# Attention and feed-forward on one core: two sets of scores at a chunk's end, a softmax one slot sooner, an output block added by GpSimd

## The chip, the core and the metric

The kernel runs on one NeuronCore of a Trainium2 chip. Its engines are TensorE (PE, with its weight loads as PEld), VectorE (DVE), ScalarE (ACT), GpSimd (POOL) and SyncE (SP), which issues most of the DMAs. Each engine works through its own instructions in order. The metric is the device time of one execution in microseconds (us), the median over runs.

## What is computed

```python
block, window = (32, 16)
k_sum = k.reshape(B, H, nb, block, D).max(axis=3)
v_sum = v.reshape(B, H, nb, block, D).mean(axis=3)
scores_l = scale * np.matmul(q, k.transpose(0, 1, 3, 2))
mask_l = np.abs(pos[:, None] - pos[None, :]) < window
scores_s = scale * np.einsum('bhsd,bhnd->bhsn', q, k_sum) + np.log(block)
a = softmax(concat(where(mask_l, scores_l, -1e9), scores_s))
x = matmul(a, concat(v, v_sum))        # then heads side by side: 3072 x 512
h = np.maximum(x @ w_in, 0.0)
out = h * h @ w_out                    # 512 -> 2048 -> 512
```

There are 4 batches, 8 heads, 768 positions and a head size of 64, all in fp32. Each query sees its neighbours within 16 positions and one key and value for each block of 32.

## The kernel before

The 3072 tokens are 24 tiles of 128. Two tiles make a chunk of 256 tokens, so there are 12 chunks. A chunk's attention gives x (two halves, high and low part of each number), and the feed-forward of the chunk runs while the attention of the next chunk's two tiles, called a and a + 1, is made beside it.

The program has three parts. A START table of tokens, written out by hand, orders the work of the first chunks. Chunks 2 and 3 run through `slot` and `period`. Chunks 4 to 11 run through `chunk_blocks`, which holds most of the change.

`chunk_blocks(c)` has 8 slots, k = 0 to 7. A slot computes two 128-wide pieces of the first layer on PE (`ffn1`, L419, 24 matmuls into `ph`), then the second layer for the slot two before (`ffn2_blocks`, L650, 21 matmuls). The second layer uses a scheme with seven products in place of eight; its operands are made by `squares_blocks` (relu L427 and square L660 on ACT, L662 on ACT, L664 to L670 on POOL, L671 on DVE) and `split_blocks` (L675 on ACT, L676 on POOL). POOL also issues the loads of the summed weights into a ring (`load_t`, L619).

Beside this the lists `early[k]` and `late[k]` put attention steps into the slots. They run ahead of and behind `split_blocks` of their slot:

- `scores(g)` (L288): 16 matmuls of a 64x64 array form, each in two passes, into banks 0 and 1 of PSUM, for each tile g from 10 on the same two banks.
- `mask_max(g, h)` (L316, DVE): adds the mask to head h's scores, keeps the maximum, writes `e_sb`. Eight heads.
- `exponentials` (L324, ACT), `sharpen` and `norm` (L341, L351, L356, DVE), `turn` (L369, DVE): softmax and transposes into `pT`.
- `outputs(g)` (L387): 16 matmuls of 64 columns into `ph`'s banks, each in two passes; `high_x` (L401, ACT) and `low_x` (L404, DVE) split the result into x. `split_x` is both.
- `load_qk`, `load_v`, `place_k` bring the keys, queries and values of later tiles.

At a chunk's end `outputs` of both tiles and `scores` of the next chunk's first tile run, then the last two `ffn2_blocks`, and then `evict_blocks` adds the seven products into four output blocks (ACT copies one operand, DVE adds, SP stores). The scratch for it is `c11`, `c22`, `c12`, `c21`, which lie in the tiles `k_sb[0]` and `q_sb[0]`. `s_flat` is the tile `q_sb[2]`.

Of the kernel before, what the change touches and what calls it, by code (L numbers as in the profile page):

```python
# [20 lines left out]
B, H, S, D = 4, 8, 768, 64  # L21
# [11 lines left out]
FROM_BLOCKS = 4  # L33
# [33 lines left out]
SU14v F1.11.0 SH15 AD15 RE10a MU10 E5.0 CA15a SU15v F1.11.1 E5.2 E5.3 SQ10 GL10 F2.10.0 F2.10.1 RE11v SQ11 MU11 GL11  # L67
F2.11.0 F2.11.1 EP5.0v TT5.7 L:kw3 TT5.6 RE12a MU12 VT3 E5.7 SQ12 NR5.0p GL12 E5.5 F1.14.0 E5.6 L:q6 EP5.1p NR5.1v
N5.1v KT3 L:v5 L:kw0 L:v4 L:q7 L:k7 F1.15.0 EV2.0a L:o0 F1.14.1 N5.0p RE13a SQ13 MU13 EV2.1v L:o1 F2.12.0 GL13 TU5.2
RE14v TU5.0 MU14 F2.12.1 F2.13.0 F1.15.1 F2.13.1 SQ14 KT0 RE15a PK6a GL14 F2.14.0 F2.14.1 VT0 TU5.1 O5 O4 XH5 XL5 MU15  # L70
PK7a XH4 SQ15 XL4 GL15 S6.0 S6.1 S7.0 S7.1
"""


# [1 line left out]
def attn_ffn_kernel(ctx: ExitStack, tc: tile.TileContext, q, k, kt, v, vt, v0, w, consts, out, out_rows):  # L76
# [231 lines left out]
    def mask_max(g, h):  # L308

        t = g % NT  # L310
        m = mask_sb[:, 0 if t == 0 else 2 if t == NT - 1 else 1, :]
        half, i = divmod(h, 4)
        if (g, half) not in nmx:
            nmx[g, half] = work.tile([P, 4], F32, name="nmx", tag="nmx", bufs=7)
            sm[g, half] = work.tile([P, 4], F32, name="sm", tag="sm", bufs=7)
        nc.vector.tensor_tensor_reduce(  # L316
            out=e_of(g)[:, h, 0:NK], in0=s_ps[g][h % 2][:, h // 2, 0:NK], in1=m, scale=-scale, scalar=3.0e38,
            op0=ALU.add, op1=ALU.min, accum_out=nmx[g, half][:, i : i + 1],
        )

    def exponentials(g, h):
        half, i = divmod(h, 4)
        e = e_of(g)[:, h, 0:NK]
        nc.scalar.activation(  # L324
            e, e, AF.Exp, bias=nmx[g, half][:, i : i + 1], scale=-1.0, accum_out=sm[g, half][:, i : i + 1]
        )

    def softmax(g, h0, h1):

        for h in range(h0, h1):  # L330
            mask_max(g, h)
            exponentials(g, h)
# [21 lines left out]
    def norm(g, half, eng):  # L354
        e = e_of(g)[:, half * 4 : half * 4 + 4, 0:NK]
        eng.tensor_mul(out=e, in0=e, in1=sm.pop((g, half)).unsqueeze(2).to_broadcast([P, 4, NK]))  # L356
# [21 lines left out]
    def outputs(g):  # L378
        if g < FROM_PAIRS:
            held["O", g] = free.pop(0)  # L380
        xp = bank[held["O", g] if g < FROM_PAIRS else 5 - g % 2 if g < 2 * FROM_BLOCKS + 2 else 4 + g % 2]
        x_ps[g] = xp = xp.rearrange("a (p k) -> a p k", p=NPAIR)

        for s in range(2):
            for h in range(H):
                o = (h % 2) * 64
                nc.tensor.matmul(  # L387
                    xp[o : o + 64, h // 2, s * 64 : s * 64 + 64],
                    lhsT=v_sb[g % 2][:, s, h * 64 : h * 64 + 64],
                    rhs=pT[g % 2][:, h, s * 64 : s * 64 + 64],  # L390
                    start=True, stop=True,
                )
# [7 lines left out]
    def high_x(g):  # L400
        nc.scalar.copy(out=x_part(xh, "xh", g), in_=x_ps[g])  # L401

    def low_x(g):
        nc.vector.tensor_sub(out=x_part(xl, "xl", g), in0=x_ps.pop(g), in1=x_part(xh, "xh", g).bitcast(F32))  # L404
        if g < FROM_PAIRS:
            free.append(held.pop(("O", g)))

    def split_x(g):
        high_x(g)
        low_x(g)  # L410
# [114 lines left out]
    def sharpen(g, half):  # L525
        add_eps(g, half, nc.vector)
        inverse(g, half)
# [150 lines left out]
    def evict_blocks(c):  # L678


        mid, side = ob_last
        c11, c22, c12, c21 = side[:, 0:CT], side[:, CT:], mid[:, 0:CT], mid[:, CT:]
        o = (c - FROM_BLOCKS) * CT
        to = [out_rows[at : at + P, x : x + CT] for at in (o + P, o) for x in (0, CT)]
        x1, x2 = ([acc[i][:, h * CT : (h + 1) * CT] for h in range(2)] for i in (1, 2))
        x0, x3 = [acc[0][:, h * CT : (h + 1) * CT] for h in range(2)], acc[3][:, 0:CT]
        nc.scalar.copy(out=c21, in_=x1[1])
        nc.vector.tensor_add(out=c11, in0=x1[0], in1=c21)
        nc.sync.dma_start(out=to[0], in_=c11)
        nc.vector.tensor_add(out=c22, in0=x0[0], in1=c21)  # L690
        nc.vector.tensor_add(out=c21, in0=x0[1], in1=c22)
        nc.vector.tensor_add(out=c22, in0=x2[0], in1=c22)
        nc.vector.tensor_add(out=c12, in0=x2[1], in1=c22)
        nc.sync.dma_start(out=to[1], in_=c12)
        nc.vector.tensor_add(out=c22, in0=x3, in1=c22)
        nc.sync.dma_start(out=to[3], in_=c22)
        nc.vector.tensor_add(out=c21, in0=x3, in1=c21)
        (nc.scalar if c == n_c - 1 else nc.sync).dma_start(out=to[2], in_=c21)

    def chunk_blocks(c):  # L700
        a = 2 * c + 2
        more, next_too = a < n_g, a + 2 < n_g
        b, t = divmod(a, NT)
        early, late = [[] for _ in range(SLOTS)], [[] for _ in range(SLOTS)]
        if more:
            for h in range(2):
                early[0] += [lambda h=h: sharpen(a, h), lambda h=h: norm(a, h, nc.vector)]
            late[0].append(lambda: turn(a, 0, 3))
            early[1].append(lambda: turn(a, 3, 6))
            late[1] += [lambda: turn(a, 6, 7), lambda: load_v(a), lambda: load_v(a + 1)]  # L710
            early[2].append(lambda: turn(a, 7, 12))
            late[3] += [lambda h=h: mask_max(a + 1, h) for h in range(H)]
            for n in range(2):
                early[4 + n] += [lambda h=h: exponentials(a + 1, h) for h in range(4 * n, 4 * n + 4)]
            for h in range(2):
                early[4 + h] += [lambda h=h: sharpen(a + 1, h), lambda h=h: norm(a + 1, h, nc.vector)]
            late[5].append(lambda: turn(a + 1, 0, 5))
            early[6].append(lambda: turn(a + 1, 5, 9))
            late[6].append(lambda: turn(a + 1, 9, 12))
            if c == FROM_BLOCKS:  # L720
                for p in range(1, 4):
                    late[2 * p - 2].append(lambda p=p: load_kv(3, p))
                    (late[2], early[4], late[6])[p - 1].extend([lambda p=p: sum_k(3, p), lambda p=p: sum_v(3, p)])
            if b and t == 0:
                late[4] += [lambda: place_v(a, nc.scalar), lambda: place_v(a + 1, nc.scalar)]
            if next_too:
                late[3].append(lambda: load_qk(a + 2))
                late[4].append(lambda: load_qk(a + 3))
                late[5].append(lambda: place_k(a + 2, nc.scalar))
                late[6].append(lambda: place_k(a + 3, nc.scalar))  # L730
        for k in range(SLOTS):
            n = (c - FROM_BLOCKS) * SLOTS + k
            ph = bank[4 + k % 2]
            for i in range(2):
                ffn1(c, 2 * k + i, ph[:, i * CT : (i + 1) * CT])
            if n == 0:
                done = finish()
            if k == 3 and more:
                scores(a + 1, 0, NPAIR)
            if k > 1:  # L740
                ffn2_blocks(n - 2)
            squares_blocks(n, ph)
            if k > 1:
                load_t(n if n < SLOTS else n + 1)
            if n == 0:
                for h in range(2):
                    evict(*done, h, nc.scalar)
                    store(done[0], h)
                load_t1(SLOTS - 1)
            for do in early[k]:  # L750
                do()
            if k == SLOTS - 1 and more:
                outputs(a)
                outputs(a + 1)
                high_x(a)
            split_blocks(n)
            for do in late[k]:
                do()
        if more:
            if next_too:  # L760
                scores(a + 2, 0, NPAIR)
            low_x(a)
            split_x(a + 1)
            if next_too:
                softmax(a + 2, 0, H)
        ffn2_blocks(n - 1)
        ffn2_blocks(n)
        if n < SLOTS:
            load_t(n + 1)
        load_t(n + 2)  # L770
        load_t(n + 3)
        evict_blocks(c)
# [228 lines left out]
```

## Time and profile before

| what | us |
|---|---|
| median of 3 runs | 587.94 (587.77 to 588.04) |
| the profiled execution | 588.17 |
| its span, first to last instruction | 586.4 |
| PE busy in it | 573.3 |
| DVE, ACT, POOL busy | 397.1, 336.9, 361.1 |

The granted TensorE clock was full through the span. The span starts with the first instruction and ends with the last; the execution's own time has 1.8 us more around it. A busy share is an average over the parts of the program. What sets the time is read from the places where one engine waits for another, and from the chain of work that ended last, of which PE is 89%. A timeline row gives the start of a group of equal instructions, its length from first start to last end, the engine, the line and the shapes. Matmuls overlap each other by a little, so the spacing of two groups is read from their starts.

### The profile page before, as it was taken

What the parts mean: (1) busy time and instruction counts of PE and PEld (TensorE: products, weight loads), DVE (VectorE), ACT (ScalarE), POOL (GpSimd) and SP (SyncE); (2) the same over time, 40 slices, a digit from 0 to 9 for tenths busy, and PEclk for the clock granted to TensorE, in tenths of its full rate; (3) what the DMA queues carried; (4) which work ended last, traced back from release to release, by engine and by line L of the source; (5) the groups of instructions that cost most, each with busy time, mean ns of one, the idle gap of its engine ahead of it and who ended that gap; (6) DMA issues with size and microseconds to landing.
All of it is one profiled execution on the core that took longest, in us unless ns stands there. A gap on an engine that the chain in (4) does not pass through costs nothing.

```text
span 586.4 us, 15654 instructions
## 1 busy us (share of the span) xinstructions
PE 573.3 (98%) x6239; PEld 563.5 (96%) x6239; DVE 397.1 (68%) x1087; ACT 336.9 (57%) x822; POOL 361.1 (62%) x430
## 2 busy tenths in 40 slices
PE   7899999999999999999999999999999999999996
PEld 6789999999999999999999999999999999999996
DVE  6899797969978946676665665764756656655212
ACT  3898857345445536565575664565475575573552
POOL 2646644405776765764874874873875784675684
PEclk9999999999999999999999999999999999999999
DMA  8999800654467658978647556646656655455362
GB/s 297 371 345 414 355 2 10 222 174 164 162 206 234 195 159 257 301 253 300 203 157 240 194 176 201 208 169 213 212 172 199 219 201 163 150 192 172 104 212 92
DMA packets 42986, 121.23 MB, mean 207 GB/s; under 512 B 3936, under 2 KB 20320, under 8 KB 41376
## 3 DMA queue, kind: packets, MB, share of 16 engines
q1 hardware_dynamic: 31376, 67.66, 33.0%
q0 software_dynamic: 11392, 52.43, 27.4%
q8 instruction: 49, 0.80, 0.5%
q14 instruction: 25, 0.20, 0.1%
q10 hardware_dynamic: 144, 0.13, 0.1%
HBM read 105.53 MB, written 14.68 MB: 205 GB/s over the span
## 4 chain that ended last, share of the span: by engine, by line
PE 89%; DMA 6%; POOL 1%; DVE 1%; ACT 1%; SPq 1%; issue 0%; DVEq 0%; POOLq 0%
PE ph L419 39%; PE o_ps L464 15%; PE o_ps L650 15%; PE s_ps L650 10%; PE ph L387 4%; DMA v_sb<-in_v 3%; PE s_ps L288 3%; PE s_ps L419 3%; DMA t_ring<-t 1%; DMA c_sb<-in_consts 1%; POOL sets L676 0%; POOL q_sb L664 0%; PE s_ps L387 0%; POOL q_sb L670 0%; SPq L190 0%
## 5 line engine op out<-in xcount | busy, mean ns | idle before, releaser
L419 PE MATMUL ph<-x,w_sb 128*128 128x256 f32 x1848 | 220.6, 275 | 0.0
L419 PEld LDWEIGHTS ph<-x,w_sb 128*128 128x128 f32 x1848 | 214.6, 188 | 0.3 <-issue 0.3
L671 DVE TENSOR_TENSOR sets<-r,sets 128x384 fp32r<-128x384 f32 x64 | 49.7, 777 | 99.6 <-ACT sets L662 99.5
L369 DVE STREAM_TRANSPOSE pT<-e_sb 32x256 f32<-32x256 f32 x228 | 99.6, 437 | 4.0
L676 POOL TENSOR_TENSOR sets<-q_sb,sets 128x512 fp32r<-128x512 f32 x64 | 84.2, 1316 | 18.9 <-ACT sets L675 16.3
L427 ACT ACTIVATE r<-ph 128x512 f32<-128x512 f32 x85 | 50.7, 596 | 74.2 <-PE ph L419 72.8
L464 PE MATMUL o_ps<-sq,w_sb 128*128 128x256 f32 x768 | 92.2, 275 | 0.0
L464 PEld LDWEIGHTS o_ps<-sq,w_sb 128*128 128x128 f32 x768 | 89.4, 188 | 0.2
L675 ACT CAST sets<-q_sb 128x512 fp32r<-128x512 f32 x64 | 39.8, 622 | 78.9 <-POOL q_sb L670 77.8
L664 POOL TENSOR_TENSOR q_sb<-r 128x256 f32<-128x256 f32 x64 | 47.4, 740 | 51.7 <-ACT r L660 49.2
L324 ACT ACTIVATE e_sb<-e_sb,nmx 128x120 f32<-128x120 f32 x176 | 67.4, 384 | 12.7 <-DVE nmx L316 12.7
L650 PE MATMUL s_ps<-w_sb,sets 128*128 128x256 f32 x384 | 64.2, 275 | 0.0
L650 PE MATMUL o_ps<-w_sb,sets 128*128 128x256 f32 x384 | 56.3, 281 | 0.0
L650 PEld LDWEIGHTS s_ps<-w_sb,sets 128*128 128x128 f32 x384 | 53.1, 188 | 0.0
L650 PE MATMUL o_ps<-t_ring,sets 128*128 128x256 f32 x270 | 52.5, 276 | 0.2 <-DMA t_ring<-t 0.2
L264 POOL TENSOR_TENSOR w_raw<-w_raw 128x1024 int32<-128x1024 int32 (+1 forms) x20 | 33.1, 1660 | 30.8 <-DVE w_raw L259 13.1
L650 PEld LDWEIGHTS o_ps<-w_sb,sets 128*128 128x128 f32 x384 | 49.1, 188 | 2.1 <-issue 2.1
L600 POOL TENSOR_TENSOR f<-f,sq 128x1024 fp32r<-128x1024 f32 x8 | 19.3, 2418 | 41.4 <-ACT sq L599 41.4
L669 POOL TENSOR_TENSOR q_sb<-r,q_sb 128x128 f32<-128x128 f32 x64 | 41.1, 643 | 5.0
L660 ACT ACTIVATE r<-r 128x512 f32<-128x512 f32 x64 | 40.7, 635 | 2.0
L619 POOL DMA_DIRECT2D t_ring<-t x45 | 25.4, 564 | 26.2 <-PE o_ps L650 19.8
L650 PEld LDWEIGHTS o_ps<-t_ring,sets 128*128 128x128 f32 x270 | 40.6, 188 | 0.4 <-DMA t_ring<-t 0.4
(127 smaller groups left out, 938.6 us busy)
## 6 DMA issues: line engine op xcount, KB each, us to landing
t_ring<-t POOLq DMA_DIRECT2D x45, 768.0 KB, 4.7
t_room<-t POOLq DMA_DIRECT2D x19, 768.0 KB, 4.6
w_raw<-in_w SPq DMA_DIRECT2D x12, 1024.0 KB, 13.8
v_sb<-in_v SPq DMA_DIRECT2D x22, 384.0 KB, 6.0
k_sb<-in_k SPq DMA_DIRECT2D x19, 384.0 KB, 5.6
kv<-in_kt SPq DMA_DIRECT2D x16, 384.0 KB, 3.7
q_sb<-in_q SPq DMA_DIRECT2D x24, 256.0 KB, 4.8
kv<-in_vt SPq DMA_DIRECT2D x12, 384.0 KB, 5.0
```

The source lines that it names most:

```text
L324: nc.scalar.activation(e, e, AF.Exp, bias=nmx[g, half][:, i : i + 1], scale=-1.0, accum_out=sm[g, half][:, i : i + 1])
L369: nc.vector.transpose(out=pT[g % 2][j * 32 : j * 32 + 32, :, i * 32 : i * 32 + 32], in_=e_sb[i * 32 : i * 32 + 32, :, j * 32 : j * 32 + 32],)
L419: nc.tensor.matmul(ph, lhsT=w_sb[f][:, w, cc * P : (cc + 1) * P], rhs=x[c][:, cc, :], start=(n == 0), stop=(n == 3 * NC4 - 1))
L427: nc.scalar.activation(r, ph, AF.Relu)
L464: nc.tensor.matmul(o_ps[c][b][:, i * CT : (i + 1) * CT], lhsT=w_sb[f][:, w, d : d + P], rhs=g_, start=(first and n == 0 and i == 0), stop= ...
L650: nc.tensor.matmul(acc[b][:, half * CT : (half + 1) * CT], lhsT=operand(n, x, i), rhs=right(n, name, y), start=(first and b not in banks[: ...
L660: nc.scalar.activation(r, r, AF.Square)
L664: nc.gpsimd.tensor_tensor(out=s_flat[:, 0 : 2 * P].rearrange("p (a b) -> p a b", a=2), in0=r0.unsqueeze(1).to_broadcast([P, 2, P]), in1=r[ ...
L669: nc.gpsimd.tensor_sub(out=s2, in0=r2, in1=s0)
L671: nc.vector.tensor_sub(out=l, in0=r[:, P:], in1=h.bitcast(F32))
L675: nc.scalar.copy(out=h, in_=s_flat)
L676: nc.gpsimd.tensor_sub(out=l, in0=s_flat, in1=h.bitcast(F32))
```

## The change

Four things are done.

1. In chunks 4 to 9 the scores of both tiles of the next chunk are computed at the chunk's end: the first tile's in slot 7, ahead of the two outputs, with its eight mask steps at once; the second tile's behind the two outputs. Until now the second tile's stood in slot 3 of the next chunk. Chunk 4's own second tile goes from slot 3 to slot 2. The split of the outputs into x comes behind all of this.
2. The second tile's masks, exponentials, norms and transposes are listed one slot sooner.
3. In START the token PK7a (the copy of the key maxima for tile 7) comes directly behind PK6a.
4. In the last chunk one of the four output blocks is made by an ACT copy and a GpSimd addition in place of a DVE addition; the results lie in `s_flat`.

```diff
--- before.py
+++ after.py
@@ -67,8 +67,8 @@
 SU14v F1.11.0 SH15 AD15 RE10a MU10 E5.0 CA15a SU15v F1.11.1 E5.2 E5.3 SQ10 GL10 F2.10.0 F2.10.1 RE11v SQ11 MU11 GL11
 F2.11.0 F2.11.1 EP5.0v TT5.7 L:kw3 TT5.6 RE12a MU12 VT3 E5.7 SQ12 NR5.0p GL12 E5.5 F1.14.0 E5.6 L:q6 EP5.1p NR5.1v
 N5.1v KT3 L:v5 L:kw0 L:v4 L:q7 L:k7 F1.15.0 EV2.0a L:o0 F1.14.1 N5.0p RE13a SQ13 MU13 EV2.1v L:o1 F2.12.0 GL13 TU5.2
-RE14v TU5.0 MU14 F2.12.1 F2.13.0 F1.15.1 F2.13.1 SQ14 KT0 RE15a PK6a GL14 F2.14.0 F2.14.1 VT0 TU5.1 O5 O4 XH5 XL5 MU15
-PK7a XH4 SQ15 XL4 GL15 S6.0 S6.1 S7.0 S7.1
+RE14v TU5.0 MU14 F2.12.1 F2.13.0 F1.15.1 F2.13.1 SQ14 KT0 RE15a PK6a PK7a GL14 F2.14.0 F2.14.1 VT0 TU5.1 O5 O4 XH5 XL5 MU15
+XH4 SQ15 XL4 GL15 S6.0 S6.1 S7.0 S7.1
 """
 
 
@@ -683,6 +683,7 @@
         o = (c - FROM_BLOCKS) * CT
         to = [out_rows[at : at + P, x : x + CT] for at in (o + P, o) for x in (0, CT)]
         x1, x2 = ([acc[i][:, h * CT : (h + 1) * CT] for h in range(2)] for i in (1, 2))
+        spare = s_flat[:, CT:]
         x0, x3 = [acc[0][:, h * CT : (h + 1) * CT] for h in range(2)], acc[3][:, 0:CT]
         nc.scalar.copy(out=c21, in_=x1[1])
         nc.vector.tensor_add(out=c11, in0=x1[0], in1=c21)
@@ -690,9 +691,15 @@
         nc.vector.tensor_add(out=c22, in0=x0[0], in1=c21)
         nc.vector.tensor_add(out=c21, in0=x0[1], in1=c22)
         nc.vector.tensor_add(out=c22, in0=x2[0], in1=c22)
-        nc.vector.tensor_add(out=c12, in0=x2[1], in1=c22)
-        nc.sync.dma_start(out=to[1], in_=c12)
-        nc.vector.tensor_add(out=c22, in0=x3, in1=c22)
+        if c == n_c - 1:
+            nc.scalar.copy(out=c12, in_=x2[1])
+            nc.gpsimd.tensor_add(out=spare, in0=c12, in1=c22)
+            nc.sync.dma_start(out=to[1], in_=spare)
+        else:
+            nc.vector.tensor_add(out=c12, in0=x2[1], in1=c22)
+            nc.sync.dma_start(out=to[1], in_=c12)
+        u, c22 = c22, c22 if c < n_c - 1 else s_flat[:, 0:CT]
+        nc.vector.tensor_add(out=c22, in0=x3, in1=u)
         nc.sync.dma_start(out=to[3], in_=c22)
         nc.vector.tensor_add(out=c21, in0=x3, in1=c21)
         (nc.scalar if c == n_c - 1 else nc.sync).dma_start(out=to[2], in_=c21)
@@ -709,14 +716,14 @@
             early[1].append(lambda: turn(a, 3, 6))
             late[1] += [lambda: turn(a, 6, 7), lambda: load_v(a), lambda: load_v(a + 1)]
             early[2].append(lambda: turn(a, 7, 12))
-            late[3] += [lambda h=h: mask_max(a + 1, h) for h in range(H)]
+            late[2] += [lambda h=h: mask_max(a + 1, h) for h in range(H)]
             for n in range(2):
-                early[4 + n] += [lambda h=h: exponentials(a + 1, h) for h in range(4 * n, 4 * n + 4)]
+                early[3 + n] += [lambda h=h: exponentials(a + 1, h) for h in range(4 * n, 4 * n + 4)]
             for h in range(2):
-                early[4 + h] += [lambda h=h: sharpen(a + 1, h), lambda h=h: norm(a + 1, h, nc.vector)]
-            late[5].append(lambda: turn(a + 1, 0, 5))
-            early[6].append(lambda: turn(a + 1, 5, 9))
-            late[6].append(lambda: turn(a + 1, 9, 12))
+                early[3 + h] += [lambda h=h: sharpen(a + 1, h), lambda h=h: norm(a + 1, h, nc.vector)]
+            late[4].append(lambda: turn(a + 1, 0, 5))
+            early[5].append(lambda: turn(a + 1, 5, 9))
+            late[5].append(lambda: turn(a + 1, 9, 12))
             if c == FROM_BLOCKS:
                 for p in range(1, 4):
                     late[2 * p - 2].append(lambda p=p: load_kv(3, p))
@@ -735,7 +742,7 @@
                 ffn1(c, 2 * k + i, ph[:, i * CT : (i + 1) * CT])
             if n == 0:
                 done = finish()
-            if k == 3 and more:
+            if k == 2 and more and c == FROM_BLOCKS:
                 scores(a + 1, 0, NPAIR)
             if k > 1:
                 ffn2_blocks(n - 2)
@@ -749,20 +756,22 @@
                 load_t1(SLOTS - 1)
             for do in early[k]:
                 do()
-            if k == SLOTS - 1 and more:
-                outputs(a)
-                outputs(a + 1)
-                high_x(a)
+            if k == SLOTS - 1 and next_too:
+                scores(a + 2, 0, NPAIR)
+                for h in range(H):
+                    mask_max(a + 2, h)
             split_blocks(n)
             for do in late[k]:
                 do()
         if more:
+            for g in (a, a + 1):
+                outputs(g)
             if next_too:
-                scores(a + 2, 0, NPAIR)
-            low_x(a)
-            split_x(a + 1)
-            if next_too:
-                softmax(a + 2, 0, H)
+                scores(a + 3, 0, NPAIR)
+            for g in (a, a + 1):
+                split_x(g)
+            for h in range(H if next_too else 0):
+                exponentials(a + 2, h)
         ffn2_blocks(n - 1)
         ffn2_blocks(n)
         if n < SLOTS:
```

**PE at a chunk's end.** `ph` holds the outputs and `s_ps` the scores; `k_sb_73` and `k_sb_74` are the keys of the first and the second tile. Before, in chunk 4:

```order
L650 MATMUL s_ps<-t_ring,sets 128x256
L650 MATMUL o_ps<-t_ring,sets 128x256
L387 MATMUL ph<-pT_81,v_sb_75 64x64 x16
L387 MATMUL ph<-pT_82,v_sb_76 64x64 x16
L288 MATMUL s_ps<-k_sb_73,q_sb_77 64x120 x16
L650 MATMUL o_ps<-w_sb,sets 128x256 x6
```

Now, at the same place:

```order
L650 MATMUL s_ps<-t_ring,sets 128x256
L650 MATMUL o_ps<-t_ring,sets 128x256
L288 MATMUL s_ps<-k_sb_73,q_sb_77 64x120 x16
L387 MATMUL ph<-pT_81,v_sb_75 64x64 x16
L387 MATMUL ph<-pT_82,v_sb_76 64x64 x16
L288 MATMUL s_ps<-k_sb_74,q_sb_78 64x120 x16
L650 MATMUL o_ps<-w_sb,sets 128x256 x6
```

The first tile's scores moved ahead of the outputs, and the second tile's came in behind them from the next chunk's slot 3.

**DVE in START.** `ksum` holds the maxima over key blocks, `ph` and `s_ps` banks of PSUM, `x` the split outputs:

```order
 L198 TENSOR_REDUCE ksum_87<-kv 128x24
 L140 COPY k_sb_73<-ksum_87 128x192
+L140 COPY k_sb_74<-ksum_87 128x192
 L441 TENSOR_TENSOR sq<-s_ps,sq 128x512
 L203 TENSOR_REDUCE vsum_84<-kv 128x24
```

```order
 L404 TENSOR_TENSOR x<-s_ps,x 128x4x128
 L438 TENSOR_TENSOR ph<-ph,r 128x512
-L140 COPY k_sb_74<-ksum_87 128x192
 L404 TENSOR_TENSOR x<-ph,x 128x4x128
 L441 TENSOR_TENSOR sq<-ph,sq 128x512
```

The copy for tile 7 moved ahead past nine instructions, to directly behind the one for tile 6.

**DVE and ACT at the very end.** `s_ps_94` and `s_ps_95` are the banks with the products of `x2` and `x3`, `q_sb2_79` is `s_flat`. The rows name the semaphores that an instruction waits for. DVE now:

```order
L691 TENSOR_TENSOR q_sb0_77<-o_ps_3215,k_sb0_73 128x256 [waits DMAHW0_49,PE_49]
L692 TENSOR_TENSOR k_sb0_73<-o_ps_3215,q_sb0_77 128x256 [waits DVE_49]
L693 TENSOR_TENSOR q_sb0_77<-s_ps_94,q_sb0_77 128x256 [waits DVE_49,PE_49]
L702 TENSOR_TENSOR q_sb2_79<-s_ps_95,q_sb0_77 128x256 [waits DVE_49,PE_49,Pool_49]
L704 TENSOR_TENSOR k_sb0_73<-s_ps_95,k_sb0_73 128x256
```

ACT now:

```order
L662 CAST sets_3111<-r_85 128x384 [waits Activation_49]
L675 CAST sets_3111<-q_sb2_79 128x512 [waits Pool_49]
L688 COPY k_sb0_73<-o_ps_3216 128x256 [waits DMAHW1_49,PE_49]
L695 COPY k_sb0_73<-s_ps_94 128x256 [waits DMAHW7_49,DVE_49]
L705 DMA out_1<-k_sb0_73 128x256 [waits DVE_49]
```

One DVE addition between L693 and L702 is gone, and ACT's new copy from bank `s_ps_94` (L695) waits for DVE; the value it waits for is the end of L693.

## Rows read from the trace of the kernel before

**Rows 1.** The page, part 1: busy time, share of the span, instructions of PE.

```profile
PE 573.3 (98%) x6239; PEld 563.5 (96%) x6239; DVE 397.1 (68%) x1087; ACT 336.9 (57%) x822; POOL 361.1 (62%) x430
```

**Rows 2.** Timeline of PE, chunk 5: start us, us, engine, line, operation.

```profile
280.06 2.89 PE L419 MATMUL ph<-x,w_sb 128*128 128x256 f32 x24
282.87 1.05 PE L288 MATMUL s_ps<-k_sb,q_sb 64*64 64x120 f32 x32
...
286.38 2.89 PE L419 MATMUL ph<-x,w_sb 128*128 128x256 f32 x24
...
291.50 2.89 PE L419 MATMUL ph<-x,w_sb 128*128 128x256 f32 x24
```

**Rows 3.** Timeline of all engines around 125 us, idle time before in brackets.

```profile
123.65 0.69 DVE L404 TENSOR_TENSOR x<-s_ps,x 128x512 fp32r<-128x512 f32 x1 [1.83 <-ACT x L401]
...
123.85 1.05 PE L288 MATMUL s_ps<-k_sb,q_sb 64*64 64x120 f32 x32
...
124.85 0.25 DVE L140 COPY k_sb<-ksum 128x192 f32<-128x192 f32 x1
125.02 0.68 DVE L404 TENSOR_TENSOR x<-ph,x 128x512 fp32r<-128x512 f32 x1
125.16 0.82 PEld L288 LDWEIGHTS s_ps<-k_sb,q_sb 64*64 64x64 f32 x32 [0.49 <-DVE k_sb L140]
...
126.14 3.02 PE L419 MATMUL ph<-x,w_sb 128*128 128x256 f32 x24
```

**Rows 4.** Timeline of PE, the end of chunk 4.

```profile
261.38 0.28 PE L650 MATMUL o_ps<-t_ring,sets 128*128 128x256 f32 x1
261.58 2.08 PE L387 MATMUL ph<-pT,v_sb 128*64 128x64 f32 x64
263.60 1.05 PE L288 MATMUL s_ps<-k_sb,q_sb 64*64 64x120 f32 x32
264.57 0.97 PE L650 MATMUL o_ps<-w_sb,sets 128*128 128x256 f32 x6
...
269.50 8.33 PE L419 MATMUL ph<-x,w_sb 128*128 128x256 f32 x72
```

**Rows 5.** Timeline of PE, the end of chunk 10.

```profile
533.78 2.08 PE L387 MATMUL ph<-pT,v_sb 128*64 128x64 f32 x64
535.79 0.98 PE L650 MATMUL o_ps<-w_sb,sets 128*128 128x256 f32 x6
```

**Rows 6.** Timeline around 125 us: first and last of sixteen mask rows.

```profile
126.22 0.27 DVE L316 CUSTOM_DVE_ANT_0 e_sb<-s_ps,c_sb 128x120 f32<-128x120 f32 x1
...
127.83 0.09 DVE L316 DVE_READ_ACCUMULATOR2_ANT nmx<- 128x1 f32 x1
```

**Rows 7.** Timeline of all engines, slot 7 of chunk 5.

```profile
306.95 2.09 PE L387 MATMUL ph<-pT,v_sb 128*64 128x64 f32 x64
307.32 0.56 DVE L671 TENSOR_TENSOR sets<-r,sets 128x384 fp32r<-128x384 f32 x1
```

**Rows 8.** Timeline of all engines, the last 15 us.

```profile
575.31 0.64 ACT L660 ACTIVATE r<-r 128x512 f32<-128x512 f32 x1
...
576.09 0.74 POOL L664 TENSOR_TENSOR q_sb<-r 128x256 f32<-128x256 f32 x1 [1.06 <-ACT r L660]
...
580.13 0.37 ACT L687 COPY k_sb<-o_ps 128x256 f32<-128x256 f32 x1 [1.36 <-PE o_ps L650]
...
581.85 0.42 DVE L692 TENSOR_TENSOR q_sb<-s_ps,q_sb 128x256 f32<-128x256 f32 x1
...
583.29 0.33 SPq L696 DMA_DIRECT2D out<-q_sb  x1
583.63 0.37 ACTq L698 DMA_DIRECT2D out<-k_sb  x1
```

**Rows 9.** Timeline of POOL and PE in chunk 4.

```profile
241.18 0.57 POOL L619 DMA_DIRECT2D t_ring<-t  x1
...
249.41 0.62 PE L650 MATMUL o_ps<-t_ring,sets 128*128 128x256 f32 x3 [0.22 <-DMA t_ring<-t]
```

## The prediction

> **What bounds the kernel now.** I read the page's part on engines first: TensorE (PE) is busy for 98% of the span [rows 1]. Busy time of a pipelined engine proves little, so I went on to PE's timeline in chunks 4 to 11. There each group of matmuls starts where the one before it ends. No other engine is late in a steady chunk, and the time is the sum of PE's own stretches plus a head and a tail. A change can therefore gain only by making PE's stretches shorter, or at one of the few places where PE does wait. It loses where it makes PE wait. The profiled execution took 588.17 us (span 586.4, 1.8 around it). The median of the runs is 587.94. I form differences and take them off the median.
>
> **Scores moved to the chunk's end.** In the timeline of [rows 2] a slot without scores takes 291.50 - 286.38 = 5.12 us for 24 + 21 = 45 matmuls, 0.114 each. The slot with the second tile's scores takes 286.38 - 280.06 = 6.32. One set of scores in mid-chunk thus costs 1.20. What is in it: the scores' own weight loads run for 0.82, and the next full-array matmul starts 0.98 after they began (125.16 to 126.14), so 0.16 is a gap [rows 3]. In front lies 0.08 (282.87 - 280.06 less 24 x 0.114). The remaining 0.14 is spread over the first matmuls behind.
>
> The chunk's end [rows 4] runs from 261.49 (261.38 plus one matmul) to 269.50. Less 42 matmuls at 0.114 (4.78) that is 3.23. It holds a lead of 0.09, both outputs at 2.02, one set of scores at 0.97, and 0.15 of slow restart. Mid-chunk and end together cost 4.43 per chunk.
>
> After the change, the end is scores, two outputs, scores. It is the old end plus 0.82 plus a gap g between the first scores and the outputs, because lead, last gap and restart are paid once. For g the trace has no row. From below it is 0: the scores start with no gap behind the outputs [rows 4], and so do the blocks (535.79 - 533.78 = 2.01) [rows 5]. From above it is 0.30, the 0.16 gap and the 0.14 restart together. I take 0.16, since that row, too, is scores followed by a full-height matmul. The end is then 3.23 + 0.98 = 4.21, and the gain 4.43 - 4.21 = 0.22. Six chunks (4 to 9) fetch the next chunk's second scores this way; chunk 4's own stay in mid-chunk, one slot sooner. **6 x 0.22 = 1.32 us gained**, with ends 0.5 (g 0.30) and 2.3 (g 0).
>
> The Trainium skill, page "TensorEngine Tiling (Array Packing)", section "Key Properties", says that each change of tiling mode drains TensorE. The changes of mode go from five to four per chunk (scores 64x64, outputs 128x64, the rest 128x128). The rows agree for scores, and show no drain behind the outputs. What a uniform price would make of it is the second rival.
>
> **Does PE wait for the second scores?** Both sets use banks 0 and 1, so the second must wait for all eight mask steps of the first, which now stand in DVE's queue between slot 7's subtraction (L671) and the two L404. The masks start 1.06 after their scores do (125.16 to 126.22), and the last read ends at 127.92, which is 2.76 after [rows 3, 6]. PE reaches the second scores 0.82 + 0.16 + 2.02 = 3.00 after the first began. L671 ends 0.93 after PE enters the end (307.88 against 306.95) even behind a backlog of transposes, which the change takes out of slot 7 [rows 7]. So the masks just fit, with 0.2 to spare, and I cost this wait at 0. Uncovered, each 0.1 costs 0.6 over six chunks. The outputs' split (ACT copy, L404) comes about 1 us later, and the next chunk's first matmul is two blocks (4.8 us) away, so this is hidden. The moved exponentials, norms and transposes come a slot sooner for an output that is needed at slot 7. They lie beside PE.
>
> **The key copy at the start.** PE's weight load waits 0.49 for DVE's copy of the keys' maxima (L140), at 125.16 [rows 3]. The copy moves ahead by nine DVE instructions and is ready long before. What is late next: the second tile's bank must be read out (L404, 123.65 + 0.69 = 124.34, before PE arrives at 124.67), and x must be split. That second L404 starts right behind the square once the copy (0.17) is gone, and ends near 125.5 (125.02 - 0.17 + 0.68); the first layer's third matmul would need it at 125.65 + 0.23. In its new place the copy makes DVE's next instructions 0.17 later, at worst the outputs too. I take **0.49 gained**, with ends 0.3 (those 0.17 paid by PE) and 0.5.
>
> **The last output block.** Its DVE chain loses one addition (0.42), but three steps replace it. ACT copies x2[1] (0.37), after DVE's addition from the same bank (the last rows of the order name that wait). That addition stands where 581.85 + 0.42 = 582.27 is now. Then GpSimd adds: 576.09 - (575.31 + 0.64) = 0.14 to start and 0.74 for 256 columns. 582.27 + 0.03 + 0.37 + 0.14 + 0.74 = 583.55. SyncE issues this store and behind it the third, at about 583.95. Before, the last issue was ACT's at 583.63 [rows 8]. **0.32 lost**; from below a gain of 0.4 (if only DVE's chain counted), from above a loss of 0.6 (an addition slowed by DVE beside it). The Trainium skill, page "PSUM — Partial Sum Buffer", section "PSUM bank collisions raise a hardware error", says that ACT and DVE must not read one bank's quadrant at once. No run here shows that; by it the copy's wait cannot be left out. With the wait the tail is 0.32 longer, without it about even.
>
> **Chunk 4's transfers.** PE waits 0.22 there for a weight ring (249.41), issued by GpSimd at 241.18, while SyncE loads keys and values [rows 9]. After: slot 3's relu is later, as the scores stand ahead of its first layer, so GpSimd issues some 0.3 later. SyncE's transfers wait for a sum on DVE that now stands behind eight masks (8 x 0.2 = 1.6). So this ring gets ahead of them. I cost it at 0, ends a gain of 0.22 and a loss of 0.7.
>
> **Sum:** -1.32 - 0.49 + 0.32 = -1.49. 587.94 - 1.49 = 586.45, say **586.4 us** (588.17 becomes 586.7).
>
> **Rivals.**
> 1. *The masks come late and PE waits at each chunk's end.* For it: only 0.2 to spare, and one wait for the whole set. Against it: DVE has nothing else in slot 7, and the mask's pitch is steady at 0.2. A wait of 0.1 gives 587.0, one of 0.3 gives 588.2. It decides at 0.45: past that six waits of 0.45 or more (2.7) outweigh the gain, and at 0.5 the kernel is **slower**, 589.4. The masks would have to start 0.7 late.
> 2. *Every change of array form costs the same.* The part that is neither scores nor outputs is 1.20 - 0.82 + 3.23 - 2.02 - 0.82 = 0.77 for five changes, 0.154 each. One is saved, in six chunks: 0.92 instead of 1.32, so 586.85. Against it: rows 4 and 5 show no gap behind outputs.
> 3. *Chunk 4's ring and the tail both at their bad ends:* 0.7 + 0.3 more, 587.4. For it: the ring's landing is already the longest of its kind.
>
> **How the numbers follow.** Forecast 0.62, first rival 0.14 (0.05 of it beyond the deciding point), second 0.12, third 0.12. A measurement of this kernel can tell 0.2% from no change, 1.18 us: faster means under 586.76, slower over 589.12. The forecast's own range is that of g, its widest end: 586.45 - 0.96 to 586.45 + 0.84, so 585.5 to 587.3. I give four fifths of it to times under 586.76: 0.50. The second rival adds a third of its chance, 0.04, the first and third 0.03: faster 0.57. Slower is the first rival's far part, 0.05. The rest is 0.38. The range to hold 8 in 10 keeps the low end and takes in the third rival and the first up to a wait of 0.2: 585.5 to 587.6.
>
> **What would show it.** Right: chunk ends near 4.2 with no slot above 5.12 in chunks 5 to 10; outputs starting about 0.98 after the scores; no DVE wait on PE's L288 rows; PE's rows after 125 some 0.5 sooner; SyncE's last store issued after ACT's. Wrong: PE idle before the second scores with L316 as releaser, a gap behind the first scores well over 0.3, longer waits on the weight ring, or a tail shorter than before.

## The result: slower by 1.4%, and where the profile after shows it

| what | before | after |
|---|---|---|
| median, us | 587.98 (587.77 to 588.04, 4 runs; the first three gave the 587.94 above) | 596.11 (594.32 to 597.06, 4 runs) |
| ratio to before, 95% interval | | 1.0136 [1.0121, 1.0151] |
| the profiled execution | 588.17 | 597.06 |
| its span | 586.4 | 595.3 |

I had forecast 586.4, in a range from 585.5 to 587.6. The page's part on engines of the kernel after answers to [rows 1]: PE is busy 4.0 us longer for the same 6239 instructions, so part of the loss is matmuls that became longer. The second row is the granted TensorE clock in 40 slices; two of them later in the span (and the second) are no longer full.

```profile
PE 577.3 (97%) x6239; PEld 567.2 (95%) x6239; DVE 398.1 (67%) x1086; ACT 337.2 (57%) x823; POOL 360.8 (61%) x431
...
PEclk9899999999999999999998999999998999999999
```

I measure a chunk's end as in the prediction: from the end of the last L650 to the next L419, less 42 matmuls of 0.1133. Before, it is 3.25 in each of the chunks 4 to 9. After, it is

| chunk | 4 | 5 | 6 | 7 | 8 | 9 |
|---|---|---|---|---|---|---|
| end, us | 4.24 | 8.67 | 4.23 | 4.23 | 8.70 | 4.23 |

Four ends are, within 0.03, what I had forecast (4.21). Chunks 5 and 8 cost 4.44 and 4.47 more, 8.9 together, which is the result. They are the two chunks that run `place_v` (`b and t == 0`, every sixth tile): four DVE transposes (L215) and three ACT copies (L140) in slot 4.

PE's timeline of the kernel after, first an undisturbed end (chunk 6), which answers to [rows 4]:

```profile
356.23 0.28 PE L650 MATMUL o_ps<-t_ring,sets 128*128 128x256 f32 x1
356.44 1.05 PE L288 MATMUL s_ps<-k_sb,q_sb 64*64 64x120 f32 x32
357.42 2.09 PE L387 MATMUL ph<-pT,v_sb 128*64 128x64 f32 x64
359.43 1.05 PE L288 MATMUL s_ps<-k_sb,q_sb 64*64 64x120 f32 x32
360.41 0.97 PE L650 MATMUL o_ps<-w_sb,sets 128*128 128x256 f32 x6
...
365.33 0.85 PE L419 MATMUL ph<-x,w_sb 128*128 128x256 f32 x6
```

and then the end of chunk 5:

```profile
306.65 0.28 PE L650 MATMUL o_ps<-t_ring,sets 128*128 128x256 f32 x1
306.86 1.05 PE L288 MATMUL s_ps<-k_sb,q_sb 64*64 64x120 f32 x32
307.84 1.15 PE L387 MATMUL ph<-pT,v_sb 128*64 128x64 f32 x32
309.18 1.15 PE L387 MATMUL ph<-pT,v_sb 128*64 128x64 f32 x32 [0.19 <-ACT r L427]
312.55 2.00 PE L288 MATMUL s_ps<-k_sb,q_sb 64*64 64x120 f32 x32 [2.21 <-DVE nmx L316]
314.48 1.65 PE L650 MATMUL o_ps<-w_sb,sets 128*128 128x256 f32 x6
...
320.19 1.07 PE L419 MATMUL ph<-x,w_sb 128*128 128x256 f32 x8
```

From the first scores to the second it is 2.99 in chunk 6 and 5.69 in chunk 5: **2.70 of waiting**, 0.33 of it for the relu that frees the second tile's output bank, 2.37 for the masks (the row has 2.21 of it as idle time). From there to the next L419 it is 5.90 and 7.64: **1.74 of slower matmuls**. Together 4.44. The view of stretches of the kernel after tells why they are slower (columns: stretch, its length, busy time and instructions of PE, PEld, DVE, ACT and POOL, granted clock, DMA share, GB/s):

```profile
310.00:312.00 2.00, 0.33 (x12) 0.19 (x8) 1.63 (x10) 0.38 (x2) 1.76 (x3) 1.00 0.83 297
...
313.00:314.00 1.00, 1.00 (x27) 1.00 (x22) 0.91 (x2) 1.00 (x5) 0.95 (x1) 0.50 0.56 147
...
316.00:317.00 1.00, 1.00 (x9) 1.00 (x9) 0.00 (x0) 0.57 (x4) 0.00 (x0) 0.86 0.00 0
```

PE idles, and behind the idle time the granted clock is 0.50, the lower of its two levels (1.2 GHz), from about 313 to 316. In chunk 8 it is the same, from about 453 to 456.

Why were the masks late? The view of waits (us in total, times, longest) has two rows that matter, here of the kernel after:

```profile
ACT v_sb L140 <- DVE v_sb L215: 10.9, 3, 3.8
...
PE s_ps L288 <- DVE nmx L316: 4.4, 2, 2.2
```

Before, the first of them was 6.4 in total and 3.4 at most, and the second did not exist. The timelines of DVE and ACT in chunk 5, before:

```profile
293.75 1.26 DVE L215 STREAM_TRANSPOSE v_sb<-vsum 32x128 f32<-32x128 f32 x4
295.05 1.66 ACT L140 COPY v_sb<-v_sb 32x512 f32<-32x512 f32 x3 [1.51 <-DVE v_sb L215]
296.73 0.60 ACT L427 ACTIVATE r<-ph 128x512 f32<-128x512 f32 x1
...
300.96 0.59 ACT L427 ACTIVATE r<-ph 128x512 f32<-128x512 f32 x1
...
305.24 0.59 ACT L427 ACTIVATE r<-ph 128x512 f32<-128x512 f32 x1
```

and after:

```profile
294.87 2.23 DVE L369 STREAM_TRANSPOSE pT<-e_sb 32x256 f32<-32x256 f32 x5
297.11 1.26 DVE L215 STREAM_TRANSPOSE v_sb<-vsum 32x128 f32<-32x128 f32 x4
298.41 1.65 ACT L140 COPY v_sb<-v_sb 32x512 f32<-32x512 f32 x3 [3.76 <-DVE v_sb L215]
300.08 0.60 ACT L427 ACTIVATE r<-ph 128x512 f32<-128x512 f32 x1
...
303.55 0.62 ACT L675 CAST sets<-q_sb 128x512 fp32r<-128x512 f32 x1 [1.65 <-POOL q_sb L670]
...
308.54 0.59 ACT L427 ACTIVATE r<-ph 128x512 f32<-128x512 f32 x1
...
310.37 0.71 DVE L671 TENSOR_TENSOR sets<-r,sets 128x384 fp32r<-128x384 f32 x1 [3.49 <-PE ph L387]
311.00 0.27 DVE L316 CUSTOM_DVE_ANT_0 e_sb<-s_ps,c_sb 128x120 f32<-128x120 f32 x1
```

The change put five of the second tile's transposes (L369, 2.23) into `late[4]`, in a line that stands ahead of `place_v`. DVE does them first, so L215 ends 2.23 later, the copies that need it wait on ACT, and ACT takes its instructions in order: the relu of slot 5 (L427) stands behind the copies, and with it the whole path of the following slots. (The Trainium skill, page "TensorE: Matmul & The Clock Gate", section "Architectural detail: the array is 16× 32×32, not 1× 128×128", says that ScalarE and VectorE keep strict order; the rows agree, the relu starting 0.02 behind the copies.) The loop of ACT and POOL (L675 waits for POOL, as in the row at 303.55, and the next relu comes behind it) then goes at its own pace, 4.28 a slot (300.96 to 305.24 before). PE's slot is 5.12, so a delay shrinks by some 0.8 a slot and is not gone by slot 7. There the relu, its square, L671 (310.37) and eight masks follow each other, and the second scores wait for the last mask. The second set of scores starts 312.55 - 308.54 = 4.01 after that relu.

### The profile page after: what moved, and what is told of

It is laid out like the page before. It is cut to its first block, busy times and chain, and to the rows that moved or that the text cites. A ratio compares the mean times of both kernels' runs of the same rounds, so it can differ in the third digit from the quotient of the medians.

```text
span 595.3 us, 15645 instructions
## 1 busy us (share of the span) xinstructions
PE 577.3 (97%) x6239; PEld 567.2 (95%) x6239; DVE 398.1 (67%) x1086; ACT 337.2 (57%) x823; POOL 360.8 (61%) x431
## 4 chain that ended last, share of the span: by engine, by line
PE 79%; POOL 6%; ACT 4%; DMA 4%; DVE 3%; issue 2%; SPq 1%; POOLq 0%; DVEq 0%
PE ph L419 33%; PE o_ps L464 15%; PE o_ps L650 12%; PE s_ps L650 8%; PE s_ps L419 3%; PE ph L387 3%; PE s_ps L288 3%; POOL q_sb L664 2%; DMA vn<-in_v 2%; POOL q_sb L669 1%; POOL sets L676 1%; DMA t_ring<-t 1%; POOL q_sb L670 1%; ACT r L427 1%; DMA c_sb<-in_consts 1%
## 5 line engine op out<-in xcount | busy, mean ns | idle before, releaser
L419 PE MATMUL ph<-x,w_sb 128*128 128x256 f32 x1848 | 220.6, 275 | 0.0
L419 PEld LDWEIGHTS ph<-x,w_sb 128*128 128x128 f32 x1848 | 214.6, 188 | 0.3 <-DVE x L404 0.2
L671 DVE TENSOR_TENSOR sets<-r,sets 128x384 fp32r<-128x384 f32 x64 | 49.3, 771 | 101.4 <-ACT sets L662 94.2
L369 DVE STREAM_TRANSPOSE pT<-e_sb 32x256 f32<-32x256 f32 x228 | 99.5, 437 | 3.9
L464 PE MATMUL o_ps<-sq,w_sb 128*128 128x256 f32 x768 | 92.6, 276 | 0.0
L675 ACT CAST sets<-q_sb 128x512 fp32r<-128x512 f32 x64 | 39.8, 621 | 90.7 <-POOL q_sb L670 90.5
L427 ACT ACTIVATE r<-ph 128x512 f32<-128x512 f32 x85 | 50.7, 596 | 70.8 <-PE ph L419 67.6
L464 PEld LDWEIGHTS o_ps<-sq,w_sb 128*128 128x128 f32 x768 | 89.5, 188 | 0.4 <-DVE sq L441 0.4
L650 PE MATMUL s_ps<-w_sb,sets 128*128 128x256 f32 x384 | 64.1, 275 | 0.0
L650 PE MATMUL o_ps<-w_sb,sets 128*128 128x256 f32 x384 | 56.9, 284 | 0.0
L650 PEld LDWEIGHTS s_ps<-w_sb,sets 128*128 128x128 f32 x384 | 53.2, 188 | 0.0
L650 PE MATMUL o_ps<-t_ring,sets 128*128 128x256 f32 x270 | 52.4, 276 | 0.2 <-DMA t_ring<-t 0.2
L650 PEld LDWEIGHTS o_ps<-w_sb,sets 128*128 128x128 f32 x384 | 50.3, 192 | 1.5 <-issue 1.4
L669 POOL TENSOR_TENSOR q_sb<-r,q_sb 128x128 f32<-128x128 f32 x64 | 39.4, 616 | 5.0
L316 DVE CUSTOM_DVE_ANT_0 e_sb<-s_ps,c_sb 128x120 f32<-128x120 f32 x176 | 38.9, 277 | 4.4 <-PE s_ps L288 3.8
```

The source lines that it names most:

```text
L369: nc.vector.transpose(out=pT[g % 2][j * 32 : j * 32 + 32, :, i * 32 : i * 32 + 32], in_=e_sb[i * 32 : i * 32 + 32, :, j * 32 : j * 32 + 32],)
L419: nc.tensor.matmul(ph, lhsT=w_sb[f][:, w, cc * P : (cc + 1) * P], rhs=x[c][:, cc, :], start=(n == 0), stop=(n == 3 * NC4 - 1))
L427: nc.scalar.activation(r, ph, AF.Relu)
L464: nc.tensor.matmul(o_ps[c][b][:, i * CT : (i + 1) * CT], lhsT=w_sb[f][:, w, d : d + P], rhs=g_, start=(first and n == 0 and i == 0), stop= ...
L650: nc.tensor.matmul(acc[b][:, half * CT : (half + 1) * CT], lhsT=operand(n, x, i), rhs=right(n, name, y), start=(first and b not in banks[: ...
L669: nc.gpsimd.tensor_sub(out=s2, in0=r2, in1=s0)
```

## The experiments

To compare kernels I count the relu's start from the start of the chunk's end on PE ("relu", in chunk 5) and look at slot 5 and slot 7. In chunk 6 after, where ACT waits for PE, slot 7's relu starts at 354.15, 2.29 ahead of 356.44: on time is -2.29. The second scores are due 2.99 to 3.00 behind the start of the end, and they start 4.01 behind the relu, so theory one says **wait = relu in slot 7 + 1.01**, where positive. After, the relu is at 308.54 - 306.86 = 1.68, and the wait 2.69 by this sum, 2.70 by the rows. Every other kernel below is a test of it. The rival theories are that the two sets of scores on two banks are the cause (then all six ends would wait, which they don't) and that the softmax a slot sooner is enough by itself.

The first four ran on a chip where the kernel before had 587.98 (median of 34 runs), the last four on one where it had 587.66 (31 runs). The ratios are the recorded ones, each with its 95% interval; they differ from the quotient of the two medians by up to 0.0016.

**1. `place_v` ahead of the transposes.** The changed kernel with one line moved:

```diff
-            late[4].append(lambda: turn(a + 1, 0, 5))
             if b and t == 0:
                 late[4] += [lambda: place_v(a, nc.scalar), lambda: place_v(a + 1, nc.scalar)]
+            late[4].append(lambda: turn(a + 1, 0, 5))
```

> The changed kernel, but in chunks 5 and 8 the placing of the block values (DVE transposes, then ACT copies) is listed ahead of the second tile's first five transposes in slot 4. Theory (ACT's queue): in the changed kernel ACT's copies wait 3.8 us on DVE in slot 4 and every later relu is late; taking the five transposes (2.2 us) out of that wait makes slot 7's relu about 2.2 us sooner, the wait of PE before the second scores falls from 2.2 to about 0.7, and the time to 587.8 if TensorE's clock stays up, 590 if it still falls. Rival (the new order at the chunk's end is slow by itself, the placing has nothing to do with it): 594 or more.

Median 588.40, ratio to before 0.9994 [0.9975, 1.0014]: against the kernel before, all but a few tenths of the loss is gone with one line. The wait left over is smaller than the 0.7 expected, the time 0.6 longer than the 587.8 expected. PE's second scores in chunk 5:

```profile
310.28 1.25 PE L288 MATMUL s_ps<-k_sb,q_sb 64*64 64x120 f32 x32 [0.42 <-DVE nmx L316]
311.46 0.98 PE L650 MATMUL o_ps<-w_sb,sets 128*128 128x256 f32 x6
```

The ends of chunks 5 and 8 are 4.93 and 4.89, the others 4.23 or 4.24. Slot 7's relu is at 306.27, the first scores at 306.80: -0.53 + 1.01 = 0.48, and the rows give 310.28 - 306.80 - 2.99 = 0.49. The six L650 behind the wait are not slow: 0.98, against 0.97 in chunk 6 after.

**2. The change without the softmax's move** (scores, START and tail as in the change):

```diff
-            late[2] += [lambda h=h: mask_max(a + 1, h) for h in range(H)]
+            late[3] += [lambda h=h: mask_max(a + 1, h) for h in range(H)]
...
-            late[4].append(lambda: turn(a + 1, 0, 5))
-            early[5].append(lambda: turn(a + 1, 5, 9))
-            late[5].append(lambda: turn(a + 1, 9, 12))
+            late[5].append(lambda: turn(a + 1, 0, 5))
+            early[6].append(lambda: turn(a + 1, 5, 9))
+            late[6].append(lambda: turn(a + 1, 9, 12))
```

> The changed kernel with the second tile's masks, exponentials, norms and transposes back in their old slots; both sets of scores stay at the chunk's end. Theory (ACT's queue): no transposes stand ahead of the placing, so the long wait goes, but the loop of ACT and GpSimd has lost the 1.2 us that the scores in slot 3 gave it, so slot 7's relu is about 1 us later than before the change: 587 to 588.5. Rival (new end order by itself): 594 or more. Rival (the softmax's earlier slots are the whole cause): 586.4.

Median 589.53, 1.0 above the range that was expected, which the ends below explain only in part; ratio 1.0014 [0.9994, 1.0034]. Chunks 5 and 8 still end in 5.02, chunk 4 in 4.38:

```profile
306.06 1.05 PE L288 MATMUL s_ps<-k_sb,q_sb 64*64 64x120 f32 x32
...
309.63 1.25 PE L288 MATMUL s_ps<-k_sb,q_sb 64*64 64x120 f32 x32 [0.51 <-DVE nmx L316]
```

So the moved scores alone bring a wait, a smaller one: 309.63 - 306.06 - 2.99 = 0.58, where the sum gives -0.55 + 1.01 = 0.46. The other 0.12 has its place in DVE's queue: the seven transposes that are back in slot 7 end at 307.58 and hold L671 until 307.60, 2.09 behind the relu, where it is 1.83 in the kernel after.

**3. The softmax's move without the change of the scores.** The kernel before, with the softmax's lines as in the change and the second tile's scores in slot 2 of every chunk:

```diff
-            if k == 3 and more:
+            if k == 2 and more:
                 scores(a + 1, 0, NPAIR)
```

> The kernel before with the second tile's softmax a slot sooner and its scores in slot 2 in place of slot 3; nothing else changed. Theory (ACT's queue): slot 7's relu is 2.2 us later in chunks 5 and 8, about as late as PE's second output needs it, a wait of 0.2 each, and nothing at the end waits for masks: 588.0 to 588.8. Rival (the softmax's earlier slots are the whole cause): 594 or more.

Median 588.08, ratio 0.9986 [0.9965, 1.0006]. The five transposes stand ahead of `place_v` here too, and cost almost nothing: the ends of chunks 5 and 8 are 3.47 and 3.49 instead of 3.25. Neither half of the change does what both do. Here is why, in chunk 5:

| kernel | relu of slot 5 | relu of slot 7 | second scores' wait |
|---|---|---|---|
| before | 296.73 - 306.95 = -10.22 | -1.71 | none there |
| softmax alone (3) | -7.96 | +0.53 | none there (0.22 for the outputs' bank) |
| scores alone (2) | -9.06 | -0.55 | 0.58 |
| both | -6.78 | +1.68 | 2.70 (0.33 of it before the second outputs) |

In slot 5 the softmax makes the relu 2.26 later, which is the five transposes, the scores 1.16, and both 3.44, so the two delays add. The 1.16 is about what a set of scores took in slot 3 (1.20): there ACT and POOL had had that time to catch up. In before the relu had 0.58 of lateness in slot 7 already (-1.71 against -2.29), and 0.70 to go before the sum -1.71 + 1.01 turns positive. 1.16 passes that by itself; 2.25 more makes 2.7.

**4. `place_v` off ACT's path.** The changed kernel with both placings in slot 6, the copies on DVE:

```diff
-                late[4] += [lambda: place_v(a, nc.scalar), lambda: place_v(a + 1, nc.scalar)]
+                late[6] += [lambda: place_v(a, nc.vector), lambda: place_v(a + 1, nc.vector)]
```

> The changed kernel with the placing of the block values moved to slot 6 and its copies given to DVE, so that ACT copies nothing there. Theory (ACT's queue): both long waits of PE go, every chunk end costs 4.2, TensorE's clock stays up, and the time is what the prediction's other terms give, 586.4. Rival (new end order by itself): 594 or more.

Median 585.97, ratio 0.9964 [0.9937, 0.9991]: 0.4% faster than the kernel before, with 1 just outside the interval. All six ends are 4.23 or 4.24, and slot 7's relu waits for PE again, at 304.32 - 306.61 = -2.29, on time:

```profile
304.32 0.60 ACT L427 ACTIVATE r<-ph 128x512 f32<-128x512 f32 x1 [0.78 <-PE ph L419]
...
306.61 1.05 PE L288 MATMUL s_ps<-k_sb,q_sb 64*64 64x120 f32 x32
...
309.60 1.05 PE L288 MATMUL s_ps<-k_sb,q_sb 64*64 64x120 f32 x32
```

**5. A delay between.** The changed kernel with two of the five transposes ahead of `place_v` and three behind:

```diff
-            late[4].append(lambda: turn(a + 1, 0, 5))
+            late[4].append(lambda: turn(a + 1, 0, 2))
             if b and t == 0:
                 late[4] += [lambda: place_v(a, nc.scalar), lambda: place_v(a + 1, nc.scalar)]
+            late[4].append(lambda: turn(a + 1, 2, 5))
```

> The changed kernel with only two of the five transposes ahead of the placing of the second tile's values, the other three behind it: a delay of ScalarE's copies between the two already run. The theory (delay on VectorE holds ScalarE's queue, the masks and so the second scores come late in chunks 5 and 8): TensorE waits there between 0.4 and 2.4 us, about 1.3 (two fifths of the way). If the clock stays at its upper level through a wait of that length, 8.9 lost before becomes about 2 x 1.3 against a wait-free chunk: 589.9 us. If the clock falls there as behind the wait of 2.4: about 1.75 more in each, 593.4 us. The rival (transposes and copies are not what decides, the wait jumps in full or not at all): 588.4 or 596.1 us.

Median 590.32, ratio 1.0036 [1.0014, 1.0059]; ends 5.81 and 5.82 in chunks 5 and 8.

```profile
305.90 1.05 PE L288 MATMUL s_ps<-k_sb,q_sb 64*64 64x120 f32 x32
...
310.28 1.25 PE L288 MATMUL s_ps<-k_sb,q_sb 64*64 64x120 f32 x32 [1.32 <-DVE nmx L316]
311.46 0.97 PE L650 MATMUL o_ps<-w_sb,sets 128*128 128x256 f32 x6
```

The wait is 1.32 where 1.3 was expected. The relu is at 306.27 - 305.90 = 0.37, so the sum gives 1.38, the rows 310.28 - 305.90 - 2.99 = 1.39. The wait grows with the delay and does not jump, so the rival falls. Chunk 8 gives the same in every kernel: by the sum 2.69 after, 0.45 in experiment 1, 0.48 in 2 and 1.39 here, by the rows 2.69, 0.46, 0.60 and 1.41. And the clock is full in every stretch from 300 to 320 of this kernel, while the six L650 take 0.97 (1.65 after):

```profile
310.00:312.00 2.00, 1.72 (x36) 1.55 (x37) 1.60 (x8) 2.00 (x8) 1.62 (x2) 1.00 0.36 95
```

**6. START alone.** The kernel before with nothing but `PK7a` moved behind `PK6a` in the table.

> The kernel before with nothing changed but the place of the key copy in the starting order. If the 0.49 us wait is all that stood there: 587.5 us, no VectorE wait on TensorE's weight loads near 125 us, first matmul behind the second scores 0.49 us sooner. The rival (the copy's new place delays what the first tile's outputs wait for): 587.8 to 588.0.

Median 587.52, ratio 0.9997 [0.9978, 1.0015]: half a us is too little for this measurement. Its trace shows both tiles' scores as one group of 64 at 122.64 and L419 1.80 behind it at 124.44, exactly as in the changed kernel. It also shows a wait 16 us later that the kernel before does not have; the section on the prediction comes back to it.

**7. The tail alone.** The kernel before with only the last output block's new lines (`spare`, the ACT copy, GpSimd's addition).

> The kernel before with nothing changed but the last output block. By the sum of the prediction 0.32 us longer, 588.3 us, with the last issue SyncE's third store some 2.7 us after the last blocks' matmul began, in place of ScalarE's at 2.34. The rival (hidden beside the other stores): 587.95.

Median 588.68, ratio 1.0014 [1.0003, 1.0024], that is 0.8 us [0.2, 1.4] longer by the ratio and 1.02 by the medians: not hidden, and by its middle dearer than the 0.32 expected, which is still inside the interval. The last issue is SyncE's third store, 2.70 behind the last blocks' matmul (581.30 to 584.00), as expected.

**8. Experiment 4 with the old tail.** Both edits above, the output block as before.

> The previous kernel (second tile's values placed by VectorE in slot 6) with the last output block in its old form. The theory that the tail costs what the traces' ends give (0.36 us): 585.6 us, the last store issued about 0.36 us sooner after the last blocks' matmuls. The rival, that the tail's new form is free beside the final transfers: no difference, 585.97. Chunk ends 4.23 in all six chunks by both.

Median 585.80, ratio 0.9971 [0.9959, 0.9983]. It beats the kernel before by 1.7 us. Against experiment 4, which ran on another chip, its ratio is not distinguishable, so the tail's price is not seen in this pair, and neither the theory nor the rival is settled by it.

## Why the prediction was wrong, step by step

**Scores moved to the chunk's end: right.** The ends without a wait are 4.23 against 4.21. Before they were 1.20 + 3.25 = 4.45, so 0.22 is gained in each, 1.32 in six. The outputs start 0.98 after the scores (356.44 to 357.42), my g of 0.16, and the second scores follow the outputs without a gap (2.01). Rival 2, one price for every change of form, would have saved 0.154; the rows side with the gap that only scores have.

**"Does PE wait for the second scores?": the step that failed.** I costed it at 0 on two grounds. One was that L671 ends 0.93 after PE enters the end "even behind a backlog of transposes, which the change takes out of slot 7". That took the backlog for the cause. It cost L671 only about 0.25: the transposes end at 307.29, and ACT's L662, which L671 also needs, ends at 307.03. In chunk 5 the relu was late itself, at 305.24, and with 4.01 from relu to second scores only 0.70 was to spare. The other was the sentence that the moved exponentials, norms and transposes "lie beside PE". They do, but in two chunks of six they moved ahead of `place_v` in DVE's queue, on which ACT waits with the relus behind it. Price: 8.9 us, the two chunk ends. I read a margin of 0.2 from START's masks and never followed one chunk with `place_v` from slot 4 to slot 7. That margin holds where the relu is on time: in chunk 6 after, the last mask's read ends at 359.25 and the second scores start at 359.43. But the 1.06 in it was right by luck. The masks at 126.22 belong to tile 6, whose scores began at 123.85 and not at 125.16, and they stand directly behind L441; in chunk 6 the masks start 357.54 - 356.44 = 1.10 after their scores. The numbers could be had from the trace of before: -1.71, and 1.20 for the scores that leave slot 3, and 2.23 for the transposes, and 1.01, make 2.73 of wait.

It is rival 1's mechanism, masks that come late, which I gave 0.14. I had it in every chunk at up to 0.5; it is 2.7 in two chunks. I had also no term for the clock. Behind that wait the matmuls took 1.74 longer per chunk, and 0.20 of that comes without a fall of the clock (1.18 from second scores to L650 in experiment 5, against 0.98). So some 1.5 per chunk, a third of the loss, is the clock.

**The key copy at the start: half right, mis-sized.** First scores to L419 was 123.85 to 126.14 [rows 3], 2.29, and is 1.80, so 0.49 is gained there. What is late next is the second L404, as foreseen, and PE's weight loads wait 0.16 for it:

```profile
124.14 1.87 PE L288 MATMUL s_ps<-k_sb,q_sb 64*64 64x120 f32 x64
...
125.94 2.81 PEld L419 LDWEIGHTS ph<-x,w_sb 128*128 128x128 f32 x24 [0.16 <-DVE x L404]
```

But most of the gain is given back 16 us later, and for that the sum had no term. On DVE's way from the scores to the square L441 only the copy is gone: L441 starts 139.85 - 123.85 = 16.00 after the first scores before and 139.98 - 124.14 = 15.84 after. PE comes 0.49 sooner, needs that square for the third group of the second layer (L464) and waits for it. Before:

```profile
139.88 2.88 PE L464 MATMUL o_ps<-sq,w_sb 128*128 128x256 f32 x24
142.60 2.88 PE L419 MATMUL ph<-x,w_sb 128*128 128x256 f32 x24
```

and after:

```profile
139.66 3.17 PE L464 MATMUL o_ps<-sq,w_sb 128*128 128x256 f32 x24
...
140.73 1.91 PEld L464 LDWEIGHTS o_ps<-sq,w_sb 128*128 128x128 f32 x16 [0.20 <-DVE sq L441]
```

The next L419 starts at 142.67, so the group takes 3.01 in place of 2.72, 0.29 more. It takes 2.98 to 3.03 in all seven kernels with the new START and 2.72 in the three with the old one. From the first scores to the scores of tile 10 (214.34 before, 214.48 after) 90.49 became 90.34: the net gain is 0.15 where 0.49 was forecast.

**The last output block: half right, mis-sized.** From the last blocks' L650 to the last issue it was 583.63 - 581.29 = 2.34 before, and it is 2.70: 0.36 longer, 0.32 forecast.

```profile
589.00 0.50 PE L650 MATMUL s_ps<-t_ring,sets 128*128 128x256 f32 x3
...
590.02 0.37 ACT L695 COPY k_sb<-s_ps 128x256 f32<-128x256 f32 x1 [1.81 <-DVE q_sb L693]
...
590.52 0.72 POOL L696 TENSOR_TENSOR q_sb<-k_sb,q_sb 128x256 f32<-128x256 f32 x1 [2.66 <-ACT k_sb L695]
590.91 0.38 ACTq L705 DMA_DIRECT2D out<-k_sb  x1
591.27 0.33 SPq L697 DMA_DIRECT2D out<-q_sb  x1
591.70 0.41 SPq L703 DMA_DIRECT2D out<-q_sb  x1
```

(ACT's copy begins as DVE's read of the same bank ends, 589.56 + 0.42; the order that the Trainium skill's page "PSUM — Partial Sum Buffer" asks for in "PSUM bank collisions raise a hardware error" is kept, and the copy's wait is in the sum.) What the sum lacked is the stores' landing. From last issue to the span's end it is 586.39 - 583.63 = 2.76 before and 595.27 - 591.70 = 3.57 after, 0.81 more. The view of DMAs over the last 8 us (KB each, median us to landing) has, for SP's three stores after:

```profile
out<-q_sb SPq DMA_DIRECT2D x3, 128.0 KB, 2.6
```

It was 1.7 before; after, the first of the three still lands in 1.7 and the last two take 2.7 and 2.6. In the profiles of the six kernels with the new tail it is 3.5 to 3.6 from last issue to end five times, and 2.80 once (experiment 4, so that there only the 0.36 was left to be seen against experiment 8); in the four with the old tail 2.76 or 2.77. The tail's term is thus 0.36 + 0.81 = 1.17 in this execution, and experiment 7 agrees (0.8 [0.2, 1.4]). Why the landing is longer was not tried, and stays open.

**Chunk 4's ring: right at 0 in this pair.** The wait of [rows 9] is gone, and its like appears two slots later:

```profile
259.76 0.62 PE L650 MATMUL o_ps<-t_ring,sets 128*128 128x256 f32 x3 [0.20 <-DMA t_ring<-t]
```

From tile 10's scores to the start of chunk 4's end the two kernels take 47.24 and 47.23. In the ten profiles this stretch varies from 46.7 to 48.1, so a price of a few tenths could not be seen in it.

**The sum as it should have been:** -1.32 + 8.91 - 0.15 + 1.17 = +8.61. The two profiled executions differ by 8.89; 0.29 of that stands ahead of 124 us already (124.14 against 123.85), where the ten profiles differ by up to 1.7 (these scores start between 122.64 and 124.32). The medians differ by 8.13.

## What to carry to other kernels

When work moves to another slot, list for each engine what it now stands in front of, and follow that to the next wait of another engine, in the rare variant of the loop as well as in the common one. An in-order engine that waits for one copy holds everything behind it. A delay of an engine off the critical path is paid only beyond its slack, so two moves that cost 0.2 and 0.8 alone cost 4.4 together; find the slack as a number (here 0.70 us) before adding delays. And a stretch that the bounding engine is relieved of is also time that the others lose: where the next one to be waited for is hardly sooner itself, as DVE at the start, most of the gain is given back there.

## What the hardware showed that I had not expected

- PE idle for 2.21 us, with 0.19 idle 1.2 us ahead of it, was followed by a granted clock of 0.50 for some 3 us, in chunk 5 and, with 2.21 and 0.18, in chunk 8; idle for 1.32 (experiment 5) or 0.42 (experiment 1) left it at 1.00. No run lies between. The Trainium skill, page "TensorE: Matmul & The Clock Gate", section "HAM oscillation — how this bites in real kernels", tells of idle gaps that bring the array back to half rate. The trace agrees that idle time does it, but the gap here is shorter than the DMA waits in the page's example.
- After a wait of 0.4 to 1.4 at full clock (experiments 1, 2 and 5), the scores take 1.25 in place of 1.05, and the L650 behind them start 0.20 later, whatever the wait's length.
- The last two 128 KB stores on SyncE's queue, of the same shape and at the same spacing, took 2.4 to 2.7 us to land in five profiles of the new tail and 1.7 to 1.8 in the sixth (experiment 4).
